# Letting a kernel's own scheduler choose the engine of its copies and relus

## The chip, the cores and the metric

The kernel runs on one core of a Trainium2 chip. A core has five engines that run side by side, each with its own in-order queue: TensorE (PE) for matmuls, VectorE (DVE), ScalarE (ACT), GpSimd (POOL) and SyncE (SP), which issues transfers here. Matmul results go to PSUM, eight banks of 128 partitions by 512 floats; everything else lives in SBUF. The metric is the time of one execution on the device, in microseconds (us), as a median of several runs. A profiled execution gives the span of the core, which is about two microseconds shorter than the measured time.

## The reference

Inputs are q, k, v of shape (4, 8, 768, 64), and four feed-forward weights. The kernel works in f16 with f32 sums.

```python
# attention: each query sees only the 6 best chunks of 32 keys
k_min, k_max = min and max of k over each chunk
ub   = sum_d max(q * k_min, q * k_max)            # upper bound of a chunk's scores
ub   = where(chunk is not in the future, ub, -1e9)
sel  = the 6 chunks of the largest ub
s    = where(sel and causal, q @ k.T / 8, -1e9)
attn = softmax(s) @ v                             # (4, 8, 768, 64)
# feed-forward with a spatial gate, on x = attn with its heads side by side, (4, 768, 512)
h    = relu(x @ w_in)                             # 1024 wide
u, v = halves of h
v_n  = (v - mean(v)) / sqrt(var(v) + 1e-6)
v_s  = w_spatial @ v_n + b_spatial                # over the 768 positions
out  = (u * v_s) @ w_out                          # (4, 768, 512)
```

## The kernel before

The kernel handles two heads at a time (a pair, 16 in all, four to a batch). For each pair there are three groups of work: `prep_ops` (transposes of keys and queries, chunk bounds, selection), `attend_ops` (scores, exponentials, attention times V, division) and, after each fourth pair, `mlp_ops` (feed-forward of a batch).

Nothing is emitted at once. Every operation is first entered with its engine, two modelled times (`occ`, how long it holds its engine, and `vis`, when its result can be seen), a priority `key` (lower is earlier) and what it reads and writes. `run` then simulates the five engines and emits the instructions in the order found:

```python
def op(self, eng, occ, vis, emit, key, r=(), w=(), take=None, drop=None, ...):
    ...                                    # dependencies from r and w
def run(self, fixed=None):
    free = {"PE": 0.8, "ACT": 2.1, "DVE": 0.8, "POOL": 1.3, "SP": 0.8}
    ...
    while left:
        best = None
        for e, lst in ready.items():
            for (k, n, t, o) in lst:       # t: when its inputs are there
                ...                        # and, if it takes a PSUM bank, when one is free
                t = max(t, free[e])
                if t < INF and (best is None or (t, k, n) < best[:3]):
                    best = (t, k, n, e, o) # earliest start, then lowest key
        ...
        if o.drop is not None:
            bank_free[j] = o.seen
```

The engine of an operation is fixed by the author. The lines that the change touches, cut to their calls:

```python
s = Schedule(banks, {"sc": 3, "tr": 2, "ub": 1, "av": 2, "mlp": 3})   # most banks of each kind

# const_ops: presets of ring buffers, and the constant rows of kh
for j in range(len(qs_r)):
    s.op("DVE", 0.8, 0.9, lambda j=j: preset(qs_r[j]), -98 + 30 * j, ...)          # L276, L277
    ...
for j in range(len(kh_r)):
    for hi in range(2):
        s.op("DVE", 0.3, 0.4, ... nc.vector.tensor_copy(kh_r[j][...], ex), -40 + 10 * j, ...)   # L303

# prep_ops(i)
s.op("PE", ..., tr_k, ...)                                     # six transposes of kp, L379
s.op("ACT", *act_cost(S), ... nc.scalar.copy(kT, bk.f16[:, 0:S]), key, ...)         # L381
...                                    # VectorE: t1, t2, kmm, chunk minima and maxima, L385 to L391
for hi in range(2):
    for par in range(2):               # spread km: VectorE if i < 2, else GpSimd, L399 and L401
        s.op("DVE" if i < 2 else "POOL", 0.2, 0.26, spread, key, ...)
for hi in range(2):
    for par in range(2):               # put kT into kh: max of a tile with itself, L409
        s.op("DVE", 0.28, 0.40, put, key + 3, ...)
s.op("PE", ..., tr_q, key + 0.3, ...)                          # L416
s.op("DVE", 0.41, 0.54, ... max(q, 0) -> rq[:, 0] ...)         # L418
s.op("DVE", 0.41, 0.54, ... max(-q, 0) -> rq[:, 1] ...)        # L421
...                                    # PE: bounds ub (L431); VectorE: mask, max8, select (L439 to L453)
# i < 5: a by six transposes on PE (L467) and a copy on VectorE (L470); later by a DMA transpose (L458)

# attend_ops(i): scores on PE (L492, triangle L495), exponentials on ScalarE (L499),
# masking of diagonal blocks on GpSimd (L507), times V on PE (L516), division on VectorE (L528),
# then x16 -> xT by PE (L544) and VectorE (L547), or by a DMA transpose (L536)

# mlp_ops(b): v = PE (L563), relu on ScalarE (L567), statistics on VectorE (L569), vn (L580)
#             u = PE (L590), relu on ScalarE (L594)
#             spatial = PE (L604), gate on VectorE (L608), gT by DMA (L612) or PE and VectorE (L619, L621)
#             out = PE (L626), copy on ScalarE (L629), DMA out (L631)

for i in range(NPAIR):
    load_ops(i, -101 if i == 0 else 10 * i - 30)
    prep_ops(i, 10 * i - (PRE if i else 50))
    attend_ops(i, 10 * i)
    ...
    if i % HP == HP - 1:
        k0 = 10 * i + 16
        mlp_ops(b, k0, k0 + 6, k0 + 14, 1.0)
```

Of the kernel before, what the change touches and what calls it, by code (L numbers as in the profile page):

```python
# [14 lines left out]
P = 128  # L15
# [42 lines left out]
class Op:  # L58
    __slots__ = ("eng", "occ", "vis", "emit", "key", "take", "drop", "deps", "left", "users", "start", "end",
                 "seen", "load", "slack", "n", "tag")  # L60


class Schedule:
# [7 lines left out]
    def op(self, eng, occ, vis, emit, key, r=(), w=(), take=None, drop=None, load=0.0, slack=0.0, tag=""):  # L71
        o = Op()
        o.eng, o.occ, o.vis, o.emit, o.key, o.take, o.drop = eng, occ, vis, emit, key, take, drop
# [15 lines left out]
        o.deps, o.left, o.users, o.start, o.end, o.seen = deps, len(deps), [], None, None, None  # L89
        for d in deps:  # L90
            d.users.append(o)
# [3 lines left out]
    def run(self, fixed=None):  # L95
# [5 lines left out]
        use = {}  # L101
        loads = 0.0
        order = []

        def push(o):
            t = 0.0
            for d in o.deps:
                t = max(t, d.end if d.eng == o.eng == "PE" else d.seen if d.eng == o.eng else d.seen + LATE)
            ready[o.eng].append((o.key, o.n, t + o.slack if o.deps else t, o))
# [4 lines left out]
        INF = 1e18  # L114
        left = len(self.ops)
        while left:
            best = None
            for e, lst in ready.items():
                for (k, n, t, o) in lst:
                    if o.take is not None:  # L120
                        c = o.take.cls
                        mine = sorted(bank_free[j] for j in range(len(holder)) if holder[j] == c)
                        cap = self.caps[c]
                        if len(mine) >= cap:
                            t = max(t, mine[len(mine) - cap])
                        t = max(t, min(bank_free))
                    t = max(t, free[e])
                    if t < INF and (best is None or (t, k, n) < best[:3]):
                        best = (t, k, n, e, o)
# [3 lines left out]
            ready[e] = [x for x in ready[e] if x[3] is not o]  # L133
            if o.take is not None:
                c = o.take.cls
# [4 lines left out]
                holder[j], bank_free[j] = c, INF  # L140
# [3 lines left out]
            o.end = t + o.occ  # L144
            o.seen = t + o.vis
            if o.load:
                loads = max(loads, o.end) + o.load
                o.seen = loads + 1.5 + (LATE_X if o.eng == "SP" else 0.0)
            free[e] = o.end
            if o.drop is not None:  # L150
                j = owner[o.drop]
                bank_free[j] = o.seen
# [7 lines left out]
        for o in order:  # L160
            o.emit()
# [23 lines left out]
def kernel(  # L185
# [31 lines left out]
    G_XBAR = 3  # L217

# [3 lines left out]
    s = Schedule(banks, {"sc": 3, "tr": 2, "ub": 1, "av": 2, "mlp": 3})  # L222
# [56 lines left out]
    def const_ops():  # L279
        s.op("DVE", 0.1, 0.2, lambda: nc.vector.memset(identity, 0.0), -100, w=["identity"])  # L280
        s.op("POOL", *pool(P), c_identity, -100.99, w=["identity"], r=["identity"])
        for j in range(2):
            s.op("DVE", 0.1, 0.2, lambda j=j: nc.vector.memset(km_r[j], 0.0), -96 + 60 * j, w=[("kmz", j)])
        s.op("DVE", 0.1, 0.2, lambda: nc.vector.memset(cmask, 0.0), -96, w=["cmask"])
        s.op("DVE", 0.1, 0.2, lambda: nc.vector.memset(tri_t, 0.0), -96, w=["tri"])
        s.op("POOL", *pool(P), lambda: nc.gpsimd.affine_select(
            out=tri_t, in_=tri_t, compare_op=Alu.is_ge, fill=NEG, base=0, channel_multiplier=-1,
            pattern=[[1, P]]), -83, r=["tri"], w=["tri"])
        s.op("DVE", 0.1, 0.2, lambda: nc.vector.memset(eps_t, 1e-6), -30, w=["eps"])
        for j in range(len(qs_r)):  # L290
            s.op("DVE", 0.8, 0.9, lambda j=j: preset(qs_r[j]), -98 + 30 * j,
                 w=[("sel", j)])
            s.op("DVE", 0.1, 0.2, lambda j=j: nc.vector.memset(v_r[j][:, :, :, D:D + 2], 1.0), -97 + 30 * j,
                 w=[("ones", j)])
        s.op("DVE", 0.86, 1.0, lambda: nc.vector.tensor_scalar(
            ex.rearrange("p (c j) -> p c j", j=CHUNK), in0=identity[0:D, 0:NCH].unsqueeze(2).to_broadcast([D, NCH, CHUNK]),
            scalar1=NEG, scalar2=None, op0=Alu.mult), -86, r=["identity"], w=["ex"])
        s.op("POOL", *pool(4), lambda: nc.gpsimd.affine_select(
            out=cmask, in_=cmask, compare_op=Alu.is_ge, fill=-1e9, base=0, channel_multiplier=1,
            pattern=[[-CHUNK, CPT]]), -84, r=["cmask"], w=["cmask"])  # L300
        for j in range(len(kh_r)):
            for hi in range(2):
                s.op("DVE", 0.3, 0.4, lambda j=j, hi=hi: nc.vector.tensor_copy(  # L303
                    kh_r[j][D * hi:D * hi + D, hi, :], ex),
                     -40 + 10 * j, r=["ex"], w=[("exrow", j, hi)])
        s.op("SP", 0.45, 2.5, lambda: nc.sync.dma_start(out=bcol, in_=moe_b_spatial.rearrange("(t p) -> p t", p=P)),
# [7 lines left out]
    def load_ops(i, key):  # L314
# [9 lines left out]
        s.op("POOL", 1.0, 0, lambda: nc.gpsimd.dma_start(out=kp, in_=view(k)), key,  # L324
             w=[("kp", i % len(kp_r))], load=PAIRB, slack=LOAD_SLACK, tag=f"ldk{i}")
        for hi in range(2):
            c0 = D * (1 - hi)
            s.op("POOL", 0.81, 0, lambda hi=hi, c0=c0: nc.gpsimd.dma_start(  # L328
                out=qs[:, :, hi, c0:c0 + D], in_=one(q, hi)), key + 0.1,
                w=[("qd", i % len(qs_r), hi)], load=PAIRB / 2, slack=LOAD_SLACK, tag=f"ldq{i}")  # L330
        s.op("POOL", 1.0, 0, lambda: nc.gpsimd.dma_start(out=vt[:, :, :, 0:D], in_=view(v)), key + 0.2,  # L331
# [4 lines left out]
    def weight_ops(key):  # L336
# [4 lines left out]
        for half in (1, 0):  # L341
            for o in range(0, NDO, 2):
                c0 = half * DH
                s.op("POOL", 0.69, 0, lambda o=o, c0=c0: nc.gpsimd.dma_start(
# [3 lines left out]
        for to in range(0, NQT, 2):  # L348
            s.op("POOL", 0.69, 0, lambda to=to: nc.gpsimd.dma_start(
# [3 lines left out]
        for o in range(0, KO, 2):  # L353
            s.op("POOL", 0.69, 0, lambda o=o: nc.gpsimd.dma_start(
# [4 lines left out]
    def spatial_ops(key):  # L359
        for so in range(NQT):  # L360
# [5 lines left out]
            s.op("PE", *pe_cost([P] * NQT), tr, key + 0.1 * so, r=["identity"] + [("ws", to) for to in range(NQT)],  # L366
                 take=bk, w=[bk])
            s.op("DVE", 0.48, 0.60, lambda so=so, bk=bk: nc.vector.tensor_copy(wsT[:, so, :], bk.f16[:, 0:S]),
                 key + 0.1 * so, r=[bk], w=[("wsT", so)], drop=bk)

    def prep_ops(i, key):
# [8 lines left out]
        s.op("PE", *pe_cost([P] * NQT), tr_k, key, r=["identity", ("kp", nk)], w=[bk], take=bk, tag=f"trk{i}")  # L380
        s.op("ACT", *act_cost(S), lambda: nc.scalar.copy(kT, bk.f16[:, 0:S]), key, r=[bk], w=[("kT", n2)], drop=bk)  # L381
        kc = kT.rearrange("d (c ch) -> d c ch", ch=CHUNK)
        t1, t2 = t1_r[n2], t2_r[n2]
        for m, op in ((0, Alu.max), (1, Alu.min)):
            s.op("DVE", 0.28, 0.40, lambda m=m, op=op: nc.vector.tensor_tensor(  # L385
                t1[:, m], in0=kc[:, :, 0:16], in1=kc[:, :, 16:32], op=op), key, r=[("kT", n2)], w=[("t1", n2, m)])
        for m, op in ((0, Alu.max), (1, Alu.min)):
            s.op("DVE", 0.16, 0.28, lambda m=m, op=op: nc.vector.tensor_tensor(
                t2[:, m], in0=t1[:, m, :, 0:8], in1=t1[:, m, :, 8:16], op=op), key, r=[("t1", n2, m)], w=[("t2", n2, m)])
        for m, op in ((0, Alu.max), (1, Alu.min)):  # L390
            s.op("DVE", 0.28, 0.40, lambda m=m, op=op: nc.vector.tensor_reduce(  # L391
                kmm[:, m, :], t2[:, m], axis=AX.X, op=op, negate=(m == 1)), key, r=[("t2", n2, m)], w=[("kmm", n2, m)])
        for hi in range(2):
            for par in range(2):
                def spread(hi=hi, par=par):
                    o = km[D * hi:D * hi + D, :, hi, :].rearrange("d m (tp r c) -> d m tp r c", r=2, c=CPT)[:, :, :, par]
                    f = kmm[D * par:D * par + D].rearrange("d m (h tp c) -> d m h tp c", h=2, c=CPT)[:, :, hi]
                    if i < 2:
                        nc.vector.tensor_tensor(o, in0=f, in1=f, op=Alu.max)  # L399
                    else:  # L400
                        nc.gpsimd.tensor_copy(o, f)  # L401
                s.op("DVE" if i < 2 else "POOL", 0.2, 0.26, spread, key, r=[("kmm", n2, 0), ("kmm", n2, 1), ("kmz", n2)],
                     w=[("km", n2, hi, par)])
        for hi in range(2):
            for par in range(2):
                def put(hi=hi, par=par):
                    o = kh[D * (1 - hi):D * (2 - hi), hi, :].rearrange("d (tp r c) -> d tp r c", r=2, c=P)[:, :, par]
                    f = kT[D * par:D * par + D].rearrange("d (h tp c) -> d h tp c", h=2, c=P)[:, hi]
                    nc.vector.tensor_tensor(o, in0=f, in1=f, op=Alu.max)  # L409
                s.op("DVE", 0.28, 0.40, put, key + 3, r=[("kT", n2)], w=[("kh", nh, hi, par)])  # L410
# [3 lines left out]
        def tr_q():  # L414
            for t in range(NQT):
                nc.tensor.transpose(bq.f16[:, t * P:(t + 1) * P], both(qs)[:, t], identity)  # L416
        s.op("PE", *pe_cost([P] * NQT), tr_q, key + 0.3, r=["identity", ("qd", nq, 0), ("qd", nq, 1)], w=[bq], take=bq, tag=f"trq{i}")
        s.op("DVE", 0.41, 0.54, lambda: nc.vector.tensor_scalar(  # L418
            rq[:, 0, P:S], in0=bq.f16[:, P:S], scalar1=0.0, scalar2=None, op0=Alu.max),
            key + 0.2, r=[bq], w=[("rq", n2, 0)])  # L420
        s.op("DVE", 0.41, 0.54, lambda: nc.vector.tensor_scalar(  # L421
            rq[:, 1, P:S], in0=bq.f16[:, P:S], scalar1=-1.0, scalar2=0.0, op0=Alu.mult, op1=Alu.max),
# [255 lines left out]
```

## Time and profile before

| | |
|---|---|
| time, median of 3 runs | 219.17 us (217.27 to 219.80) |
| span of the profiled run | 216.2 us |
| TensorE busy | 187.7 us, 87% |
| VectorE busy | 169.5 us, 78% |
| ScalarE busy | 144.8 us, 67% |
| GpSimd busy, with the issuing of loads | 104.1 us, 48% |
| moved by DMA | 27.68 MB |

Busy times are sums over the whole span, and hide that the kernel has phases: loads and the first pairs at the start, attention with feed-forward between, and the last batch's feed-forward alone at the end. So a view by stretches of the span is read before them. A row of a group gives line, engine, operation, output <- input, shapes and count, then busy time and the mean of one, then how long the engine was idle just ahead of these instructions and what ended that. L409 is line 409 of the kernel.

### The profile page before, as it was taken

What the parts mean: (1) busy time and instruction counts of PE and PEld (TensorE: products, weight loads), DVE (VectorE), ACT (ScalarE), POOL (GpSimd) and SP (SyncE); (2) the same over time, 40 slices, a digit from 0 to 9 for tenths busy, and PEclk for the clock granted to TensorE, in tenths of its full rate; (3) what the DMA queues carried; (4) which work ended last, traced back from release to release, by engine and by line L of the source; (5) the groups of instructions that cost most, each with busy time, mean ns of one, the idle gap of its engine ahead of it and who ended that gap; (6) DMA issues with size and microseconds to landing.
All of it is one profiled execution on the core that took longest, in us unless ns stands there. A gap on an engine that the chain in (4) does not pass through costs nothing.

```text
span 216.2 us, 5372 instructions
## 1 busy us (share of the span) xinstructions
PE 187.7 (87%) x1910; PEld 114.7 (53%) x1910; DVE 169.5 (78%) x604; ACT 144.8 (67%) x297; POOL 104.1 (48%) x184
## 2 busy tenths in 40 slices
PE   0269979598999899996789999999999999699991
PEld 0157867476746455654645565665555555344540
DVE  6999999799899999899899967577985422485540
ACT  2116988487879874796798793889996669374221
POOL 7999984865543683596858524125230201000000
PEclk9999999999999999999999999999999999999999
DMA  8999999998997899999999995949904644310132
GB/s 49 126 148 154 199 187 192 171 154 59 113 104 95 58 100 194 128 204 227 202 181 133 134 126 98 200 125 180 196 1 49 136 85 144 126 49 0 60 137 97
DMA packets 117306, 27.68 MB, mean 128 GB/s; under 512 B 111904, under 2 KB 114208, under 8 KB 117280
## 3 DMA queue, kind: packets, MB, share of 16 engines
q0 software_dynamic: 77200, 12.19, 79.6%
q1 hardware_dynamic: 40080, 15.15, 37.3%
q8 instruction: 15, 0.25, 0.5%
q14 instruction: 11, 0.09, 0.1%
HBM read 24.38 MB, written 6.29 MB: 142 GB/s over the span
## 4 chain that ended last, share of the span: by engine, by line
PE 59%; DVE 23%; DMA 8%; issue 4%; ACT 3%; POOL 1%; POOLq 0%; ACTq 0%; DVEq 0%
PE bank L604 12%; PE bank L492 11%; PE bank L590 8%; PE bank L563 8%; PE bank L626 7%; PE bank L516 7%; DMA vt<-in_v_dram 5%; DVE kh L409 4%; DMA a<-qs 3%; DVE m L447 3%; ACT e L499 2%; DVE t L385 2%; DVE x L528 1%; DVE rq L418 1%; DVE vn L580 1%
## 5 line engine op out<-in xcount | busy, mean ns | idle before, releaser
L499 ACT ACTIVATE e<-bank 128x512 f16<-128x512 f32 x192 | 92.8, 555 | 22.6 <-PE bank L495 10.7
L492 PE MATMUL bank<-a,kh 128*128 128x512 f16 (+3 forms) x256 | 57.3, 310 | 3.7 <-DMA a<-qs 0.8
L507 POOL TENSOR_SCALAR_AFFINE_SELECT e<-e 128x384 f16<-128x384 f16 x48 | 26.2, 545 | 57.2 <-ACT e L499 56.3
L604 PE MATMUL bank<-vn,wsT 128*128 128x512 f16 x144 | 38.1, 379 | 0.4 <-DVE vn L580 0.4
L516 PEld LDWEIGHTS <-e 128*128 128x128 f16 x672 | 28.5, 97 | 11.8 <-issue 2.4
L516 PE MATMUL bank<-vt,e 128*128 128x65 f16 x672 | 31.5, 193 | 1.3 <-POOL e L507 0.5
L492 PEld LDWEIGHTS <-kh 128*128 128x128 f16 x256 | 22.2, 99 | 18.1 <-issue 4.5
L629 ACT COPY o<-bank 128x512 f32<-128x512 f32 x24 | 14.1, 588 | 22.7 <-PE bank L626 21.6
L328 POOL DMA_DIRECT2D qs<-in_q_dram x32 | 27.0, 854 | 3.2 <-DMA a<-qs 1.1
L608 DVE SCALAR_TENSOR_TENSOR g<-bank,bcol,u 128x512 f16<-128x512 f32 x24 | 17.9, 747 | 12.4 <-PE bank L604 12.1
L409 DVE TENSOR_TENSOR kh<-kT 64x384 f16<-64x384 f16 x64 | 23.6, 369 | 2.8 <-PE bank L492 1.4
L626 PE MATMUL bank<-w_out,gT 128*128 128x512 f16 x96 | 24.5, 379 | 0.8 <-DVE gT L621 0.7
L563 PE MATMUL bank<-w_in,xT 128*128 128x512 f16 x96 | 24.3, 379 | 0.4 <-DVE xT L547 0.4
L590 PE MATMUL bank<-w_in,xT 128*128 128x512 f16 x96 | 23.6, 379 | 0.0
L381 ACT COPY kT<-bank 128x768 f16<-128x768 f16 x16 | 13.0, 811 | 11.3 <-PE bank L379 10.5
L604 PEld LDWEIGHTS <-wsT 128*128 128x128 f16 x144 | 13.0, 98 | 10.9
L331 POOL DMA_DIRECT2D vt<-in_v_dram x16 | 16.5, 1029 | 4.5 <-PE bank L431 2.7
L324 POOL DMA_DIRECT2D kp<-in_k_dram x16 | 16.7, 1043 | 3.1 <-PE bank L544 2.1
L401 POOL COPY km<-kmm 64x24 f16<-64x24 f16 x56 | 12.4, 222 | 11.9 <-DVE kmm L391 9.5
L528 DVE TENSOR_TENSOR x<-bank,rec 128x384 f16<-128x384 f32 x32 | 17.6, 549 | 0.3
L567 ACT ACTIVATE vraw<-bank 128x512 f32<-128x512 f32 x24 | 13.7, 604 | 5.9 <-PE bank L563 5.8
L569 DVE BATCH_NORM_STATS2 st<-vraw 128x6 f32<-128x512 f32 x24 | 15.5, 675 | 2.5 <-ACT vraw L567 2.4
(59 smaller groups left out, 250.4 us busy)
## 6 DMA issues: line engine op xcount, KB each, us to landing
out_dram<-o SPq DMA_DIRECT2D x24, 256.0 KB, 2.9
kp<-in_k_dram POOLq DMA_DIRECT2D x16, 192.0 KB, 5.9
qs<-in_q_dram POOLq DMA_DIRECT2D x32, 96.0 KB, 5.3
vt<-in_v_dram POOLq DMA_DIRECT2D x16, 192.0 KB, 6.0
ws_raw<-in_moe_w_spatial_dram POOLq DMA_DIRECT2D x3, 384.0 KB, 10.0
w_in<-in_moe_w_in_dram POOLq DMA_DIRECT2D x4, 256.0 KB, 6.9
w_out<-in_moe_w_out_dram POOLq DMA_DIRECT2D x2, 256.0 KB, 11.0
gT<-g SPq DMA_TRANSPOSE x18, 4.1
```

The source lines that it names most:

```text
L328: s.op("POOL", 0.81, 0, lambda hi=hi, c0=c0: nc.gpsimd.dma_start(out=qs[:, :, hi, c0:c0 + D], in_=one(q, hi)), key + 0.1, w=[("qd", i % le ...
L409: nc.vector.tensor_tensor(o, in0=f, in1=f, op=Alu.max)
L492: mm(bs.f32[:, col:col + n], lhsT=kh[:, hi, t * P:(t + 1) * P], rhs=af[:, q0 // P:(q0 + n) // P, :], start=True, stop=not dg)
L499: s.op("ACT", *act_cost(WIDTHS[g]), lambda g=g, bs=bs, e=e: nc.scalar.activation(out=e[:, BASES[g]:BASES[g] + WIDTHS[g]], in_=bs.f32[:, 0: ...
L507: nc.gpsimd.affine_select(out=o, in_=o, compare_op=Alu.is_ge, fill=0.0, base=0, channel_multiplier=-1, pattern=[[0, 3], [1, P]])
L516: mm(o[:, qi, :], lhsT=e[:, c:c + P], rhs=vt[:, hi, t, 0:D + 1], start=(part == 0 and n == 0), stop=(part == 1 and n == len(bl) - 1))
L528: nc.vector.tensor_tensor(x16[:, :, hi, :], in0=o[:, :, 0:D], in1=rec.to_broadcast([P, NQT, D]), op=Alu.mult)
L563: mm(bk.f32, lhsT=x[:, ko, t * P:(t + 1) * P], rhs=w_in_sb[:, ko, DH:DFF], start=(ko == 0), stop=(ko == NDO - 1))
L590: mm(bk.f32, lhsT=x[:, ko, t * P:(t + 1) * P], rhs=w_in_sb[:, ko, 0:DH], start=(ko == 0), stop=(ko == NDO - 1))
L604: mm(bk.f32, lhsT=wsT[:, si, t * P:(t + 1) * P], rhs=vn[:, si, :], start=(si == 0), stop=(si == NQT - 1))
L608: s.op("DVE", 0.67, 0.80, lambda t=t, bk=bk, g=g: nc.vector.scalar_tensor_tensor(out=g, in0=bk.f32, scalar=bcol[:, t:t + 1], in1=u_r[nu[t] ...
L626: mm(bo.f32, lhsT=gT[:, db, :], rhs=w_out_sb[:, db, :], start=(db == 0), stop=(db == KO - 1))
```

## The change

An operation may now be entered with a list of engines, each with its own two times. The scheduler looks at the engine on which the operation would be seen earliest, given when each engine is free, and emits it there. The aim is to take copies and relus off an engine while another is free. Beside that the feed-forward keys move up by ten (one pair), the presets of all ring buffers get the first keys, the feed-forward work may hold four banks instead of three, and the plan counts a released bank as free a quarter of a microsecond later (`LATE`).

```diff
-    def op(self, eng, occ, vis, emit, key, r=(), w=(), ...):
+    def op(self, alts, emit, key, r=(), w=(), ...):
+        o.alts = {e: (occ, vis) for e, occ, vis in (alts if isinstance(alts, list) else [alts])}
...
+                    if len(o.alts) > 1:
+                        mineend = t + o.alts[e][1]
+                        if any(f != e and max(o.at[f], free[f], now) + o.alts[f][1] < mineend for f in o.alts):
+                            continue
...
-                bank_free[j] = o.seen
+                bank_free[owner[o.drop]] = o.seen + LATE
...
+    KV, KU, KS, STEP = 26, 6, 14, 1.0
-    s = Schedule(banks, {"sc": 3, "tr": 2, "ub": 1, "av": 2, "mlp": 3})
+    s = Schedule(banks, {"sc": 3, "tr": 2, "ub": 1, "av": 2, "mlp": 4})
+    EVAC = [("DVE", 0.48, 0.60), ("ACT", 0.72, 0.87)]
+    RELU = [("ACT", 0.51, 0.65), ("DVE", 0.60, 0.74)]
+    RQ = [("DVE", 0.41, 0.54), ("ACT", 0.62, 0.76)]
+    KH = [("DVE", 0.36, 0.44), ("POOL", 0.47, 0.53), ("ACT", 0.41, 0.55)]
+    KM = [("POOL", 0.24, 0.30), ("DVE", 0.18, 0.30), ("ACT", 0.11, 0.26)]
...                                   # presets and constants
-            s.op("DVE", 0.8, 0.9, lambda j=j: preset(qs_r[j]), -98 + 30 * j,
+            s.op(("DVE", 0.4, 0.45), lambda j=j: preset(qs_r[j]), -98 + j,
-                s.op("DVE", 0.3, 0.4, lambda j=j, hi=hi: nc.vector.tensor_copy(
-                    kh_r[j][D * hi:D * hi + D, hi, :], ex),
-                     -40 + 10 * j, r=["ex"], w=[("exrow", j, hi)])
+                s.op([("ACT", 0.72, 0.87), ("DVE", 0.45, 0.58)], lambda e, j=j, hi=hi: copy(
+                    e, kh_r[j][D * hi:D * hi + D, hi, :], ex, False), -40 + 10 * j, r=["ex"], w=[("exrow", j, hi)])
...                                   # kT; likewise a, xT, wsT with EVAC, from DVE
-        s.op("ACT", *act_cost(S), lambda: nc.scalar.copy(kT, bk.f16[:, 0:S]), key, r=[bk], w=[("kT", n2)], drop=bk)
+        s.op(EVAC, lambda e: copy(e, kT, bk.f16[:, 0:S]), key, r=[bk], w=[("kT", n2)], drop=bk)
...
-                s.op("DVE" if i < 2 else "POOL", 0.2, 0.26, spread, key, ...)
+                s.op(KM, spread, key, ...)
-                s.op("DVE", 0.28, 0.40, put, key + 3, ...)
+                s.op(KH, put, key + 3, ...)
...                                   # both query relus with RQ, from DVE
...                                   # the relus of v and u and the copy of o with RELU, from ACT
-            s.op("ACT", *act_cost(512), lambda vraw=vraw, bk=bk: nc.scalar.activation(vraw, bk.f32, func=Act.Relu),
+            s.op(RELU, lambda e, vraw=vraw, bk=bk: relu(e, vraw, bk.f32),
...
-            k0 = 10 * i + 16
-            mlp_ops(b, k0, k0 + 6, k0 + 14, 1.0)
+            k0 = 10 * i + KV
+            mlp_ops(b, k0, k0 + KU, k0 + KS, STEP)
```

On VectorE a copy from SBUF is written as the maximum of a tile with itself, a copy from PSUM as a plain copy; on GpSimd and ScalarE they are plain copies.

## The prediction, made before the changed kernel ran

> **What bounds the kernel now.** I read three views: first the busy time of the engines in four stretches of the span, then the groups of instructions by shape (for the cost of one instruction), then the timeline of the first 18 us and of the tail.
>
> The stretches (columns: us, then busy time and instruction count of TensorE, its weight loads, VectorE, ScalarE and GpSimd; granted clock; DMA share; GB/s):
>
> ```profile
> 0.00:20.00 20.00, 8.67 (x76) 6.68 (x77) 17.50 (x75) 4.75 (x7) 18.80 (x27) 1.00 1.84 116
> 20.00:120.00 100.00, 89.76 (x1100) 59.50 (x1099) 94.50 (x362) 77.89 (x161) 65.57 (x120) 1.00 1.56 150
> 120.00:200.00 80.00, 77.71 (x675) 42.98 (x672) 51.86 (x161) 58.62 (x125) 19.68 (x38) 1.00 0.71 109
> 200.00:216.20 16.20, 11.51 (x70) 5.51 (x68) 5.64 (x11) 3.52 (x6) 0.00 (x0) 0.98 0.26 98
> ```
>
> The reader is to see two regimes. Up to 120 us VectorE is busy 94.5 of 100 us, with TensorE below it; from 120 us on TensorE is all but full (77.7 of 80) and VectorE is at 65%.
>
> TensorE's busy time is not its work, since a stalled matmul counts as busy. So I count columns. In the chain of waits twelve 512-column matmuls take 2.59 us, so one is 0.216 us and 1,000 columns are 0.422 us. The feed-forward part has 96 (v) + 96 (u) + 144 (spatial) + 96 (output) = 432 matmuls of 512 columns, 221,184 columns; scores 86,016; attention times V 672 x 65 = 43,680; transposes and the triangle additions 390 x 128 = 49,920; the chunk bounds 160 x 48 = 7,680. Sum 408,480 columns, 172 us at that rate. The span is 216.2, so 44 us are lost on TensorE. Counting instructions by line in each stretch puts the loss at about 16 us in the first 20, 18 us between 20 and 120, 4.5 us between 120 and 200 and 5 us in the last 16. The change can only win in these 44.
>
> What one instruction costs (columns: line, engine, operation, tiles, count | busy us, mean ns | idle before it):
>
> ```profile
> L409 DVE TENSOR_TENSOR kh<-kT 64x384 f16<-64x384 f16 x64 | 23.6, 369 | 2.8 <-PE bank L492 1.4
> L381 ACT COPY kT<-bank 128x768 f16<-128x768 f16 x16 | 13.0, 811 | 11.3 <-PE bank L379 10.5
> L401 POOL COPY km<-kmm 64x24 f16<-64x24 f16 x56 | 12.4, 222 | 11.9 <-DVE kmm L391 9.5
> L418 DVE TENSOR_SCALAR rq<-bank 128x640 f16<-128x640 f16 x16 | 7.7, 478 | 1.2 <-PE bank L416 0.7 <-ACT e L499 0.5
> L470 DVE COPY a<-bank 128x768 f16<-128x768 f16 x10 | 5.3, 547 | 0.0
> L303 DVE COPY kh<-ex 64x768 f16<-64x768 f16 x6 | 3.7, 616 | 0.1
> L567 ACT ACTIVATE vraw<-bank 128x512 f32<-128x512 f32 x24 | 13.7, 604 | 5.9 <-PE bank L563 5.8
> ```
>
> The VectorE rows hardly wait for anything (idle 0 to 3 us in a whole row): its queue is backed up, while ScalarE waits 11 us for its kT copies.
>
> The start, on VectorE, ScalarE and TensorE:
>
> ```profile
> 3.84 1.05 DVE L303 COPY kh<-ex 64x768 f16<-64x768 f16 x2
> 5.24 0.82 PE L379 MATMUL bank<-identity,kp 128*128 128x128 f16 x6 [5.24 <-DMA kp<-in_k_dram]
> 5.91 1.79 DVE L303 COPY kh<-ex 64x768 f16<-64x768 f16 x3
> 6.09 0.80 ACT L381 COPY kT<-bank 128x768 f16<-128x768 f16 x1 [4.00 <-PE bank L379]
> 7.78 0.22 DVE L276 MEMSET qs<- 128x192 uint32 x1
> 8.16 0.33 DVE L385 TENSOR_TENSOR t<-kT 128x384 f16<-128x384 f16 x1
> 16.43 0.58 PE L492 MATMUL bank<-a,kh 128*128 128x512 f16 x1 [0.63 <-DVE a L470]
> ```
>
> The first kT is complete at 6.89, but VectorE takes it up only at 8.16: constant copies and a memset that nobody needs yet are in front. The first score matmul starts at 16.43.
>
> **What the Trainium skill says.** "ScalarE: Activation LUTs", section "What ACT_TABLE_LOAD costs": an ACTIVATE with immediate scale and bias takes 186 ns + 0.833 ns per element, for any function. The trace agrees: 613 ns by that for 512 elements against 604 here. For the relu of 640 elements it gives an estimate of 719 ns alone, against 478 on VectorE. "VectorE: DVE Perf Modes", section "Why PSUM operands drop a tier": an operand in PSUM still allows two 16-bit elements a cycle, but 32-bit ones only at one. The trace agrees: 768 16-bit columns take 547 ns and 640 take 478, so 128 more cost 69 ns, 0.54 ns each. So VectorE is the faster engine for the 16-bit evacuations, and each one that moves to ScalarE costs more there than it frees. "SBUF — State Buffer", section "Who interferes with whom": a VectorE instruction with two SBUF inputs contends with a GpSimd instruction that reads SBUF. The kh copies are such instructions (written as a maximum of a tile with itself), and they spread from 332 to 616 ns in the trace, which fits; moving some of them to GpSimd makes more such meetings.
>
> **The change part by part.**
> 1. *Free choice of engine.* Movable off VectorE between 20 and 120 us (12 of the 16 pairs prepare there, 72 of 96 key transposes): kh 48 x 0.369 = 17.7; the two query relus 24 x 0.476 = 11.4; copies of a, wsT and xT about 18 x 0.546 = 9.8. Sum 38.9 of its 94.5 us. Movable off ScalarE there: kT 12 x 0.811 = 9.7, v and u relus (50 and 38 of 96 matmuls, thus 12.5 and 9.5 instructions) 22 x 0.60 = 13.2, output copies 6 x 0.588 = 3.5; so 26.4 of 77.9. GpSimd has about 34 us idle and may take kh and km, about 0.5 us for a kh copy (an estimate between km's 222 ns for 24 elements and the 545 ns of the masking of 384). If GpSimd takes some 20 kh copies, VectorE and ScalarE share (94.5 + 77.9 - 7.4) = 165 us, and ScalarE's dearer copies add about 3: 84 us each. TensorE's own work there is 82 us (100 less the loss of 18). Three engines at about 83 us in 100 can't run back to back with in-order queues; if they reach 90 to 92% of the stretch, where VectorE reached 94.5 alone, it shrinks to 91 us. Gain 9, and I take 7.5 because the loads may not follow (below).
> 2. *The start.* Of the six constant copies (3.7 us on VectorE at 616 ns) about two go to ScalarE, which is idle till 6.09; the others become two-input maxima, about 0.46 us each. VectorE is then free near 5.4, takes the first kT itself at 6.1 (0.55 instead of 0.80) and starts the chunk maxima near 6.7 instead of 8.16: 1.5 us. The query relus, at 9.53 and 10.66, may split over two engines: up to 0.5 more. But pair 1's keys land only at 10.95 whatever VectorE does, so I count 1.5 of the 2.
> 3. *Lag by ten keys more.* Feed-forward work yields to attention a pair longer. No instruction is added. TensorE's work is moved toward the end, where it fills the waits for the last pair: TensorE idles there 0.95, 0.44 and 0.51 us at 184 to 187. Gain 0.5 to 1.5; what follows the last pair, 24 + 24 + 36 + 24 matmuls of 512 columns = 23 us plus the drain, stays.
> 4. *The fourth feed-forward bank, and the later release of a bank in the plan (a quarter of a microsecond).* These change the order alone. Within the noise of the sum; I count 0.5.
> Sum: 7.5 + 1.5 + 1 + 0.5 = 10.5 us off 219.2, so 208.7; I say 208.5.
>
> **The rivals.**
> *The loads become the bound.* DMA share is 1.56 in the busy stretch, and rows of 256 bytes of input make small packets. In the first 20 us the loads of four pairs (0.59 MB each as written) move at 116 GB/s: 5 us a pair with nothing else running. At 16 pairs that is 81 us, and the weights and the transposes share the engines. If attention is to run faster, the loads have to come earlier, and they come from GpSimd's queue, which now also carries copies. In favour: one piece of the chain of waits is a V load of 10.98 us at 30.24. Against: elsewhere in the chain DMA is small, and the share falls to 0.71 afterwards. If it holds, only the start and the tail gain: 214 to 217.
> *The plan misjudges the hardware.* The order is fixed from modelled durations, in-order on each engine. A copy that goes to ScalarE behind a row of exponentials, or to GpSimd behind a 1 us load issue or a masking, comes late, and the whole chain of the pair behind it waits. For: masking waits 56 us for exponentials in the page's groups, so GpSimd stands still at places the plan must guess. Against: the plan's figures are near the trace (0.36 for kh against 0.369, 0.48 for 768 columns against 0.547). It would give 219 to 224.
> *Everything balances, better than I assume.* If the stretch falls to TensorE's own rate, as from 120 us on (77.7 of 80), the loss of 18 drops to 4: about 202.
>
> **Range and chances.** Middle 208.5. The low side is the last rival, short of its end, 201.5; the high side is the loads' case, 216. Faster by over 2% means below 214.8: I give it 0.81; within 2% 0.13; slower 0.06.
>
> **What would show it.** Right: VectorE's busy share between 20 and 120 us below 90%, ScalarE's above 80%, kh copies on two or three engines; the first score matmul near 14.5 to 15; TensorE's total of instructions unchanged and its full regime starting near 110 instead of 120; the last pair's normalisation before 178 instead of 185.2. Wrong: VectorE still over 94% (the copies stayed, or ScalarE's feed-forward relus came over in their place); waits of TensorE for loads of keys or V that are longer than now (first rival); ScalarE or GpSimd copies named as what TensorE waits for (second).

## The result and the profile after

| | time, median | runs | range |
|---|---|---|---|
| before | 219.49 us | 4 | 217.27 to 222.15 |
| changed | 207.32 us | 4 | 204.54 to 213.05 |

The ratio is 0.9398, with a 95% interval of 0.9223 to 0.9574. (All ratios here leave out executions more than 1.5% above the fastest of their kernel, two of these four and four of the six below; medians and ranges have them all.) Later, six more executions of the same kernel (e11 below) had a median of 209.33 us, 204.90 to 213.54, and a ratio of 0.9461 (0.9388 to 0.9534). By the ratios the change takes 5 to 6% off, 12 to 13 us; by the medians 12.2 us here and 8.9 in the later set (209.33 against 218.18). So a figure "against the changed kernel" below can shift by some 3 us with the executions that it is taken from. The change also widens the spread: 9 us from the fastest to the slowest, where the kernel before has 5, and under 3 in its 41 later executions.

The stretches of the changed kernel; columns as before: us, then busy time and count of TensorE, its weight loads, VectorE, ScalarE and GpSimd; granted clock; DMA share; GB/s.

```profile
0.00:20.00 20.00, 9.27 (x92) 7.23 (x93) 15.14 (x71) 10.06 (x19) 18.26 (x29) 1.00 1.68 106
20.00:120.00 100.00, 93.60 (x1137) 62.19 (x1134) 90.36 (x337) 88.62 (x195) 75.40 (x116) 1.00 1.74 156
120.00:200.00 80.00, 79.97 (x677) 44.15 (x676) 58.12 (x172) 50.31 (x108) 22.45 (x41) 1.00 0.66 114
200.00:206.30 6.30, 2.22 (x14) 0.97 (x12) 0.69 (x2) 1.76 (x3) 0.00 (x0) 1.00 0.33 125
```

Between 20 and 120 us VectorE and ScalarE now carry about the same, near 90 of 100 us each, where they had 94.5 and 77.9. From 120 to 200 us TensorE has no idle left. And the last row is 6 us long instead of 16.

Where the copies went, in the groups by shape:

```profile
L241 POOL COPY kh<-kT 64x384 f16<-64x384 f16 x42 | 22.1, 525 | 6.3 <-DVE kT L243 3.3 <-DVE rec L555 0.8 <-ACT kT L239 0.2
L239 ACT COPY kh<-kT 64x384 f16<-64x384 f16 x18 | 9.2, 509 | 5.8 <-DVE kT L243 5.5
L243 DVE COPY kT<-bank 128x768 f16<-128x768 f16 x13 | 7.2, 552 | 4.6 <-PE bank L415 4.4
L249 ACT ACTIVATE rq<-bank 128x640 f16<-128x640 f16 x16 | 10.9, 707 | 1.5 <-PE bank L449 0.9 <-DVE rq L251 0.6
L421 DVE TENSOR_TENSOR t<-kT 128x384 f16<-128x384 f16 x32 | 12.6, 422 | 0.4 <-ACT kT L239 0.2
L424 DVE TENSOR_TENSOR t<-t 128x192 f16<-128x192 f16 x32 | 9.6, 330 | 0.0
```

The count behind the shape says who got what: of 64 kh copies 42 run on GpSimd, 18 on ScalarE and 4 on VectorE; 13 of the 16 kT copies went the other way, from ScalarE to VectorE; of 32 query relus 16 are on ScalarE.

To see where the time came from I count TensorE's columns as in the prediction (1,000 columns are 0.422 us) and take them off each stretch. What is left is TensorE's loss; a matmul is counted in the stretch in which it starts. The columns of this table are the kernels of the experiments below, one profiled execution each. The last one is a second execution of the changed kernel.

| loss of TensorE, us | before | lag alone (e3) | engines fixed (e1) | old lag (e2) | changed | changed (e11) |
|---|---|---|---|---|---|---|
| 0 to 20 | 16.0 | 16.0 | 15.9 | 14.9 | 15.3 | 13.6 |
| 20 to 60 | 8.2 | 7.6 | 10.0 | 7.1 | 6.9 | 11.4 |
| 60 to 120 | 9.7 | 8.5 | 8.6 | 8.0 | 5.8 | 3.9 |
| 120 to 200 | 4.5 | 1.2 | 1.1 | 6.5 | 1.6 | 1.1 |
| after 200 | 5.4 | 4.5 | 5.4 | 4.4 | 4.3 | 4.5 |
| sum | 43.8 | 37.8 | 41.0 | 40.9 | 33.9 | 34.5 |
| last pair divided, starts at | 185.2 | 177.0 | 180.6 | 183.6 | 172.8 | 173.3 |

The prediction had the loss fall by 10.5 us; it fell by 9.9, as the span did. The two executions of the changed kernel split it quite differently between 20 and 120 us, so these two rows are best read together: 17.9 us before, 16.1 with the lag alone, 15.1 with the old lag, 18.6 with engines fixed, 12.7 and 15.3 in the changed kernel. What stands clear of such differences is the row from 120 to 200 us: 1.1 to 1.6 us with the longer lag, 4.5 and 6.5 without. (With the longer lag the later experiments have up to 2.6, and 4.0 in e4 and e7.) That the two changes need each other is to be read from the times of the experiments, more than from single rows.

### The profile page after: what moved, and what is told of

Same layout as the page of the kernel before. It is cut to its first block, busy times and chain, and to the rows that moved or that the text cites. A ratio compares the mean times of both kernels' runs of the same rounds, so it can differ in the third digit from the quotient of the medians.

```text
span 206.3 us, 5375 instructions
## 1 busy us (share of the span) xinstructions
PE 185.1 (90%) x1910; PEld 114.5 (56%) x1910; DVE 164.3 (80%) x578; ACT 150.8 (73%) x323; POOL 116.1 (56%) x184
## 4 chain that ended last, share of the span: by engine, by line
PE 62%; DMA 20%; ACT 5%; POOL 5%; DVE 4%; issue 2%; POOLq 0%; ACTq 0%
PE bank L635 13%; PE bank L523 11%; PE bank L657 10%; PE bank L621 10%; PE bank L594 7%; DMA qs<-in_q_dram 7%; PE bank L547 6%; DMA kp<-in_k_dram 6%; DMA a<-qs 4%; ACT e L530 4%; DMA gT<-g 3%; DVE vn L611 2%; PE bank L449 2%; POOL kh L241 1%; PE bank L415 1%
## 5 line engine op out<-in xcount | busy, mean ns | idle before, releaser
L523 PE MATMUL bank<-a,kh 128*128 128x512 f16 (+3 forms) x256 | 59.2, 309 | 2.2 <-DMA a<-qs 1.3
L538 POOL TENSOR_SCALAR_AFFINE_SELECT e<-e 128x384 f16<-128x384 f16 x48 | 25.6, 532 | 38.3 <-ACT e L530 37.5
L635 PE MATMUL bank<-vn,wsT 128*128 128x512 f16 x144 | 37.4, 379 | 0.0
L547 PE MATMUL bank<-vt,e 128*128 128x65 f16 x672 | 32.5, 193 | 2.3 <-ACT e L530 1.5
L239 ACT COPY o<-bank 128x512 f32<-128x512 f32 x22 | 12.9, 586 | 19.6 <-PE bank L657 15.4
L241 POOL COPY kh<-kT 64x384 f16<-64x384 f16 x42 | 22.1, 525 | 6.3 <-DVE kT L243 3.3
L657 PE MATMUL bank<-w_out,gT 128*128 128x512 f16 x96 | 24.2, 379 | 1.1 <-DMA gT<-g 1.1
L621 PE MATMUL bank<-w_in,xT 128*128 128x512 f16 x96 | 25.0, 379 | 0.0
L594 PE MATMUL bank<-w_in,xT 128*128 128x512 f16 x96 | 24.8, 379 | 0.0
L635 PEld LDWEIGHTS <-wsT 128*128 128x128 f16 x144 | 13.1, 98 | 10.9
L600 DVE BATCH_NORM_STATS2 st<-vraw 128x6 f32<-128x512 f32 x24 | 15.9, 675 | 1.8 <-ACT vraw L249 1.8
L415 PE MATMUL bank<-identity,kp 128*128 128x128 f16 x96 | 9.0, 236 | 7.1 <-DMA kp<-in_k_dram 7.1
L657 PEld LDWEIGHTS <-gT 128*128 128x128 f16 x96 | 8.9, 98 | 11.4 <-DMA gT<-g 2.1
L478 DVE MAX8 m<-bank 128x8 f32<-128x8 f32 (+4 forms) x160 | 14.4, 162 | 0.2
```

The costliest lines, as they stand in the source:

```text
L523: mm(bs.f32[:, col:col + n], lhsT=kh[:, hi, t * P:(t + 1) * P], rhs=af[:, q0 // P:(q0 + n) // P, :], start=True, stop=not dg)
L538: nc.gpsimd.affine_select(out=o, in_=o, compare_op=Alu.is_ge, fill=0.0, base=0, channel_multiplier=-1, pattern=[[0, 3], [1, P]])
L547: mm(o[:, qi, :], lhsT=e[:, c:c + P], rhs=vt[:, hi, t, 0:D + 1], start=(part == 0 and n == 0), stop=(part == 1 and n == len(bl) - 1))
L594: mm(bk.f32, lhsT=x[:, ko, t * P:(t + 1) * P], rhs=w_in_sb[:, ko, DH:DFF], start=(ko == 0), stop=(ko == NDO - 1))
L621: mm(bk.f32, lhsT=x[:, ko, t * P:(t + 1) * P], rhs=w_in_sb[:, ko, 0:DH], start=(ko == 0), stop=(ko == NDO - 1))
L635: mm(bk.f32, lhsT=wsT[:, si, t * P:(t + 1) * P], rhs=vn[:, si, :], start=(si == 0), stop=(si == NQT - 1))
```

## The experiments

Two theories stood at the start. The prediction's: the free choice of engines is the gain, and the lag a matter of 1 us. Its rival: the lag is the main part.

**e1: engines fixed.** In the changed kernel each operation is held on its engine of before (the others get a time that they never win with).

```diff
-    KH = [("DVE", 0.36, 0.44), ("POOL", 0.47, 0.53), ("ACT", 0.41, 0.55)]
+    KH = [("DVE", 0.36, 0.44), ("POOL", 0.47, 1e6), ("ACT", 0.41, 1e6)]
...                        # likewise EVAC, RELU, RQ, KM, the constant rows; kT on ScalarE
```

> The changed kernel with every copy and relu held on the engine it had before; lag, presets, bank cap and later release stay. Theory of the prediction (the free choice is worth 7.5 to 9 of the 12 us, the lag 1): it comes back to 214 to 217 us, VectorE over 93 of the 100 us between 20 and 120. Rival (the lag is the main part, the free choice a small one): 209 to 211 us.

Measured: 214.81 us (214.0 to 215.6), ratio 0.9833 (0.9780 to 0.9886). The prediction's number: with the lag in place the free choice is worth 3.7 points of ratio against the later runs of the changed kernel, 8 us. But VectorE's share, which I said would be back over 93%, was 90.8 of 100 (third number pair of the row):

```profile
20.00:120.00 100.00, 90.62 (x1088) 61.07 (x1087) 90.78 (x339) 77.66 (x162) 63.71 (x113) 0.97 1.52 147
```

So e1 is slower without VectorE being fuller than in the changed kernel (90.4). Its trace also has two lulls of TensorE of 2.6 us, at 31.6 and 104.1 us, each with 3.4 us at half clock. These do not seem to set its time: of its four executions the two with a mean clock of 0.981 took 214.8 us on average, and so did the two with 0.992.

**e2: the old lag.**

```diff
-    KV, KU, KS, STEP = 26, 6, 14, 1.0
+    KV, KU, KS, STEP = 16, 6, 14, 1.0
```

> The changed kernel with the old feed-forward keys (lag 16 instead of 26), everything else kept. Theory of the prediction: 208 to 209 us, since the lag only fills waits in the tail. Rival (lag is the main part): 213 to 217 us, with TensorE losing time again between 120 and 200 us and at the last pair.

Measured: 217.80 us (214.44 to 225.09, 20 runs), ratio 0.9886 (0.9854 to 0.9918). The rival's case, with a median just above its range: without the lag nearly the whole gain is gone. (The profiled execution, and so the table, is one of the fastest, 214.98 us.) So the lag term is the step of the prediction that fell.

The timeline of TensorE around the last pair shows what the lag buys. First e2:

```profile
183.00 0.27 PE L547 MATMUL bank<-vt,e 128*128 128x65 f16 x3 [0.41 <-POOL e L538]
184.22 0.51 PE L575 MATMUL bank<-identity,x 128*128 128x128 f16 x6 [0.95 <-DVE x L559]
184.56 0.38 PE L594 MATMUL bank<-w_in,xT 128*128 128x512 f16 x1
185.45 0.82 PE L594 MATMUL bank<-w_in,xT 128*128 128x512 f16 x3 [0.51 <-DVE xT L243]
```

Then the changed kernel at the same point:

```profile
173.58 0.59 PE L657 MATMUL bank<-w_out,gT 128*128 128x512 f16 x2
174.01 0.50 PE L575 MATMUL bank<-identity,x 128*128 128x128 f16 x6
174.34 0.59 PE L635 MATMUL bank<-vn,wsT 128*128 128x512 f16 x2
174.78 0.59 PE L594 MATMUL bank<-w_in,xT 128*128 128x512 f16 x2
```

The brackets are idle time just ahead of a row, and the changed kernel has none. Spatial and output matmuls (L635, L657) of the batch before stand between the steps of the last pair. In e2 too few of them are left. But the brackets of e2 are 1.9 us in all, as I had counted; the larger effect is the last row of the table, a last pair that is through 11 us earlier. With feed-forward work held back, pairs get TensorE first, and the work held back fills their gaps from 120 us on (loss 6.5 us in e2, 1.6 in the changed kernel).

**e3: the lag alone, in the kernel before.**

```diff
-            k0 = 10 * i + 16
+            k0 = 10 * i + 26
```

> The kernel before with nothing but the lag raised from 16 to 26. Theory of the prediction: 218 to 219 us, about 1 us gained. Rival (lag is the main part): 209 to 213 us.

Measured: 212.47 us (211.80 to 212.57), ratio 0.9724 (0.9687 to 0.9761). The rival's number again. One constant gives 6 us, nearly half of the whole, with every instruction on its old engine.

**e5 and e6: how much lag.** The same constant at 21 and at 32, in the changed kernel.

```diff
-    KV, KU, KS, STEP = 26, 6, 14, 1.0
+    KV, KU, KS, STEP = 21, 6, 14, 1.0      # e6: 32
```

> The changed kernel with the feed-forward keys half way (lag 21). Theory now (the lag leaves feed-forward matmuls over to fill TensorE while the last pairs wait for their chains, and its worth grows till enough of them are over): between the two, 208 to 213 us, the last pair's normalisation between 173 and 184 us. Rival (each set of keys is a throw of the dice for the order, and 26 a lucky one): anything from 206 to 218 us, with no relation to where TensorE idles.

> The changed kernel with a longer lag (32). Theory now: no more to fill, so 205 to 208 us, TensorE still without idle from 160 us on. Rival (lucky throw): clearly above 208 us. Third theory (more lag only moves work into the end, where nothing runs beside it): above 210 us, with a longer stretch after the last pair's normalisation.

Measured: 217.27 us (214.80 to 220.77) with 21, and 209.68 us (206.32 to 213.22) with 32, ratio 0.9509 (0.9406 to 0.9611). The longer lag behaves nearly as my theory says: the median is above 208 us, but about the changed kernel's in its later executions (209.33), with the last pair at 171.3 us and no idle from 160 us on. The half-way lag does not: it is as slow as the old one. Only the part of the theory that speaks of the end holds for it: the loss between 120 and 200 us is 6.5, 4.4, 1.6 and 1.7 us with a lag of 16, 21, 26 and 32, but with 21 another 17.0 us go between 20 and 120 us. The worth of the lag doesn't grow evenly, and part of what a setting gives is the order that it happens to yield. How large that part is stays open.

**e7: kh copies held on VectorE.**

```diff
-    KH = [("DVE", 0.36, 0.44), ("POOL", 0.47, 0.53), ("ACT", 0.41, 0.55)]
+    KH = [("DVE", 0.36, 0.44), ("POOL", 0.47, 1e6), ("ACT", 0.41, 1e6)]
```

> The changed kernel with the kh copies held on VectorE (60 of 64 had left it, 42 to GpSimd and 18 to ScalarE); all else kept, lag 26 too. If VectorE's load up to 120 us is what the free choice relieved: 60 x 0.369 = 22 us come back to it over the 16 pairs, and the time rises by 5 to 8 us, to 211 to 214. If the free choice gains through the start and the feed-forward relus instead: within 2 us of 206.

Measured: 212.38 us (211.92 to 214.44), ratio 0.9737 (0.9671 to 0.9802), so 6 us slower than the changed kernel by the ratios (0.9737 less 0.9461, of 218 us), 3 to 5 by the medians, with VectorE at 94.5 of 100 us between 20 and 120 again. That is as expected: this one class is most of what the free choice brings.

**e8: relus and output copies held on ScalarE.**

```diff
-    RELU = [("ACT", 0.51, 0.65), ("DVE", 0.60, 0.74)]
+    RELU = [("ACT", 0.51, 0.65), ("DVE", 0.60, 1e6)]
```

> The changed kernel with feed-forward relus and output copies held on ScalarE (16 of 72 had left it for VectorE). By the balance of the two engines (about 10 of ScalarE's 151 us): at most 1.5 us slower, 205.5 to 208. If freeing ScalarE for exponentials is what counts: 209 us or more.

Measured: 215.33 us (214.77 to 216.73), ratio 0.9863 (0.9806 to 0.9920). A clear miss. Sixteen instructions that move cost 9 us by the ratios, 6 to 8 by the medians. The loss of TensorE between 20 and 60 us is 13.4 us, against 6.9 in the first profile of the changed kernel, and the first relu that had moved to VectorE starts only at 55.5 us there (the first of the group u at 65.2), so the time of the relus is not what is lost there. GpSimd's timeline of e8 shows what is:

```profile
39.84 1.02 POOL L367 DMA_DIRECT2D vt<-in_v_dram  x1 [1.07 <-PE bank L526]
40.86 0.71 POOL L390 DMA_DIRECT2D w_out<-in_moe_w_out_dram  x1
42.41 0.71 POOL L390 DMA_DIRECT2D w_out<-in_moe_w_out_dram  x1 [0.85 <-DVE bank L470]
...
44.26 1.01 POOL L360 DMA_DIRECT2D kp<-in_k_dram  x1 [0.59 <-DMA ws_raw<-in_moe_w_spatial_dram]
...
46.15 0.82 POOL L364 DMA_DIRECT2D qs<-in_q_dram  x1 [0.33 <-DMA ws_raw<-in_moe_w_spatial_dram]
47.45 0.82 POOL L364 DMA_DIRECT2D qs<-in_q_dram  x1 [0.48 <-DMA kp<-in_k_dram]
48.26 1.02 POOL L360 DMA_DIRECT2D kp<-in_k_dram  x1
49.27 1.03 POOL L367 DMA_DIRECT2D vt<-in_v_dram  x1
54.09 0.83 POOL L364 DMA_DIRECT2D qs<-in_q_dram  x1 [3.79 <-DMA vt<-in_v_dram]
...
56.24 0.53 POOL L538 TENSOR_SCALAR_AFFINE_SELECT e<-e 128x384 f16<-128x384 f16 x1
```

The load of queries at 54.09 waits 3.79 us for the V load that was issued at 39.84 and took 14 us to land. It needs nothing of that V. But it is the eighth load after it, and the trace records the semaphore of each load: the 73 loads use eight of them (99 to 106) in turn, and this load waits for number 100, which that V load holds. It is so in every trace here, the kernel before included: no load starts before the eighth load ahead of it has landed, and 0.28 us more have passed. So GpSimd's queue stands still while eight of its loads are under way, by the program's own semaphores, and what is behind in the queue stands too: the masking at 56.24, which TensorE waits for. TensorE in this time (us, busy time and count, granted clock, DMA share, GB/s):

```profile
50.00:52.00 2.00, 2.00 (x27) 1.00 1.52 159
52.00:54.00 2.00, 0.24 (x8) 1.00 1.74 156
54.00:56.00 2.00, 0.00 (x0) 0.57 2.62 153
56.00:58.00 2.00, 1.17 (x7) 0.50 2.93 151
58.00:60.00 2.00, 2.00 (x16) 0.50 2.58 150
60.00:62.00 2.00, 2.00 (x19) 0.72 0.70 44
```

A lull of 4.6 us (52.24 to 56.83). The clock goes to half at 54.29, still inside it, and stays there until 61.11, so the matmuls of another 4.3 us run at half clock: a 512-column matmul takes 634 ns there instead of 379. The Trainium skill has this in "TensorE: Matmul & The Clock Gate", section "What's actually happening": after an idle window of some 3.4 us the clock goes to half, until a busy one has passed. The granted clock of 0.50 in these rows agrees. The window need not be idle throughout, though: TensorE had been idle for only 2.0 of the 3.4 us before the drop, and the measurement decides. A late load is paid for twice.

How much of e8's time this is stays open. The second profile of the changed kernel (e11) has a shorter standstill in the same place and loses 11.4 us between 20 and 60 us, yet its span is 8.2 us shorter than e8's. Of these 8.2 us only 2.0 lie between 20 and 60 us; 3.6 lie between 60 and 120 us, where the relus or the order may be the reason.

**e4: half the loads.** From pair 4 on only one of two heads of keys and V and half of the query rows are loaded; the rest of the buffers keeps old data, so the output is not the reference's.

```diff
-        ... nc.gpsimd.dma_start(out=kp, in_=view(k)), key,
+        ... nc.gpsimd.dma_start(out=kp if i < 4 else kp[:, 0], in_=view(k) if i < 4 else one(k, 0)), key,
...                        # likewise vt; qs[:, 0:3] of each head
```

> The changed kernel, from pair 4 on loading only one of the two heads' keys and V and half of the query rows (the rest of the buffers keeps old data), same order of instructions. If the loads bound the changed kernel between 20 and 120 us: 200 to 203 us, with the waits for keys and queries of 10 us gone. If they do not, and the loss is in the order and the balance of engines: within 1.5 us of 206.

Measured: 203.67 us (202.89 to 205.16), ratio 0.9336 (0.9282 to 0.9389). Against the changed kernel's later runs (0.9461) that is 2.7 us, by the medians 4 to 6. Between the theories: the loads cost some 3 us or more. But TensorE's waits for keys and queries are not gone, as the first theory had it: 7.8 us in all against 9.5, and 5.7 of them are the first load's. The spread is smaller, 2.3 us against 9 in the changed kernel, but e7 and e12, with all the loads, have only 2.5 and 1.7, so it does not show the loads' part.

**e9 and e10: weights later.** If the weights' loads stand in the pairs' way at 34 to 57 us, later ones should help. In e9 only their keys move, and that of the spatial weight's transposes; e10 does the same to e8.

```diff
-    weight_ops([22, 23, 26, 27, 28, 29, 30, 31, 32])
+    weight_ops([30, 31, 36, 37, 44, 47, 50, 64, 66])
-            spatial_ops(38)
+            spatial_ops(56)
```

> The changed kernel with the weights' load keys and the transposes of the spatial weight moved later, and nothing else. Theory (at 34 to 57 us the weights stand in front of the pairs' loads; when one of those lands late GpSimd's queue stands still, TensorE idles for some microseconds and then runs at half clock): 202 to 206 us and a narrower spread than the changed kernel's 204.5 to 213. Rival (the weights are needed anyway, and the wait moves to the first feed-forward matmuls): 206 to 210 us.

> The run with relus held on ScalarE (215.3 us), now with the weights later as well. If its 9 us came from the lull of TensorE at 52 to 56 us and the half clock after it, and not from the relus: 204 to 209 us. If the relus on ScalarE are what costs: 213 us or more.

Measured: e9 215.17 us (214.89 to 216.21), ratio 0.9882 (0.9844 to 0.9920); e10 216.36 us (211.73 to 219.24). Both misses. GpSimd's timeline of e9 shows why:

```profile
40.37 1.01 POOL L360 DMA_DIRECT2D kp<-in_k_dram  x1 [0.55 <-DMA w_in<-in_moe_w_in_dram]
56.37 0.70 POOL L390 DMA_DIRECT2D w_out<-in_moe_w_out_dram  x1 [5.21 <-DMA kp<-in_k_dram]
```

The loads changed places, and the queue stood still all the same, now 5.2 us behind keys that took 16 us to land, with TensorE idle or at half clock from 52.5 to 63.5 us. (The mean clock of the profiled execution is 0.976, those of the other five 0.971 to 0.976, so they probably had the same.) So e9 shows the full queue again, and refutes that these keys avoid it. e10 has the same lull and says nothing of the relus: whether they cost anything beside it stays open.

**e11: the changed kernel again.**

> The changed kernel unchanged, for more executions on the same chip as the two runs above: 204 to 208 us in most, some near 212; the slow ones at a lower mean clock of TensorE, if the lull at 50 us is what comes and goes.

Measured: 209.33 us (204.90 to 213.54), with only two of the six between 204 and 208. Its profiled execution has the same wait of queries for V, 2.3 us long and ending at 52.5 us. TensorE idles for 3.2 us, but its clock stays at 1.00:

```profile
52.00:54.00 2.00, 0.16 (x6) 1.00 1.80 107
54.00:56.00 2.00, 0.65 (x8) 1.00 2.22 105
```

So the changed kernel runs close to the edge at which e8 falls off. The fastest executions had a mean clock of 1.000 (204.90) and 0.999 (207.43), the slowest 0.980 (213.54); but one of 210.11 had 0.982 and one of 212.37 had 0.992. In e2, with 20 executions, it is plainer: 1.000 at 214.44 and 214.98 us, 0.972 to 0.985 in the five above 222. This fits a lull that comes and goes, but only the profiled executions show it directly.

**e12: three feed-forward banks, and banks counted free at once.**

```diff
-                bank_free[owner[o.drop]] = o.seen + LATE
+                bank_free[owner[o.drop]] = o.seen
-    s = Schedule(banks, {"sc": 3, "tr": 2, "ub": 1, "av": 2, "mlp": 4})
+    s = Schedule(banks, {"sc": 3, "tr": 2, "ub": 1, "av": 2, "mlp": 3})
```

> The changed kernel with three feed-forward banks instead of four and banks counted free at once, as before. The prediction's fourth term (0.5 us): 206 to 207.5 us. Rival (the plan without the quarter microsecond promises banks too early, and TensorE stalls on them): 209 us or more.

Measured: 210.25 us (209.39 to 211.06), ratio 0.9648 (0.9601 to 0.9694). By the ratios the two are worth 4 us here, the rival's number; by the medians of the same chip (210.25 against 209.33) it is 0.9 us. And e1 and e3 differ by these two, the presets, the plan's corrected durations and the rewritten loop of `run`, and there the kernel that has them is the slower one (0.9833 against 0.9724). So neither size nor sign is settled, and no cause is shown.

No version that ran was faster than the changed kernel with its full work.

## Why the prediction was right, and where it was not

**What bounds the kernel.** Right in the main. Taking kh copies off VectorE (e7 undoes that) is worth 6 us by the ratios, 3 to 5 by the medians. But e1 is slower than e7 with VectorE at 90.8 of 100 us, where e7 has 94.5, so VectorE's share alone does not set the time. ScalarE above 80%: 88.6. VectorE below 90%: 90.4, just missed.

**Step 1, free choice, 7.5 us.** Right in size, 8 us by e1, but only with the longer lag. With the old lag it brings 2.5 us by the ratio and 0.5 by the medians, and that with presets and banks counted in (e2). GpSimd's 0.5 us for a kh copy was 0.525. What the step left out: the copies that left slow VectorE down. The chunk maxima, which read two SBUF tiles, take 348 and 248 ns in e1:

```profile
L423 DVE TENSOR_TENSOR t<-kT 128x384 f16<-128x384 f16 x32 | 10.2, 348 | 1.0 <-ACT kT L239 0.8
L426 DVE TENSOR_TENSOR t<-t 128x192 f16<-128x192 f16 x32 | 6.9, 248 | 0.0
```

In the changed kernel they take 422 and 330, as shown above: 32 x 74 + 32 x 82 ns is 5 us of VectorE given back against e1, and 3 us against the kernel before, where they take 361 and 294. Single instructions of the changed kernel show whose doing it is: of the first kind the 12 with no GpSimd computing beside them take 367 ns on average, the 19 that overlap a kh copy on GpSimd 461; of the second kind 20 take 260 and 11 take 435. This is the contention with GpSimd's reads that the prediction named from the Trainium skill, and didn't put a number on. VectorE's busy time fell by only 5 us in all (169.5 to 164.3), for a second reason as well: some 32 us of copies and query relus left it, but 24 us came over in exchange, 13 kT copies (7.2 us), 24 more km copies (5.8) and the 16 feed-forward relus and output copies (10.9).

**Step 2, the start, 1.5 us.** VectorE takes up the first chunk maxima at 6.94, predicted near 6.7. The first scores come at 15.81 in this execution, not at 14.5 to 15. The timeline of the changed kernel:

```profile
3.51 1.67 ACT L239 COPY kh<-ex 64x768 f16<-64x768 f16 x2 [1.42 <-DVE ex L332]
6.94 0.62 DVE L421 TENSOR_TENSOR t<-kT 128x384 f16<-128x384 f16 x2
7.13 0.84 POOL L364 DMA_DIRECT2D qs<-in_q_dram  x1
8.02 1.07 POOL L241 COPY kh<-kT 64x384 f16<-64x384 f16 x2
9.03 0.83 POOL L364 DMA_DIRECT2D qs<-in_q_dram  x1
13.73 0.80 PE L449 MATMUL bank<-identity,qs 128*128 128x128 f16 x6 [1.22 <-DMA qs<-in_q_dram]
14.32 1.48 PE L498 MATMUL bank<-identity,qs 128*128 128x128 f16 x12
15.81 0.58 PE L523 MATMUL bank<-a,kh 128*128 128x512 f16 x1
```

Two kh copies on GpSimd now stand between the two query loads of pair 1. The second goes out at 9.03 instead of directly behind the first (8.10 in the kernel before), lands at 13.6, and the transposes of pair 0's selected queries (L498) stand behind pair 1's (L449) in TensorE's queue. So 0.7 us of loss was saved here. In e11 that load went out at the same time and landed at 12.4, the first scores came at 15.1 and the loss was 13.6, a gain of 2.4. So the landing makes more of a difference here than the place of the two copies. This execution is the outlier: in the ten other traces with a free choice (all but e1 and e3) the first scores come at 14.6 to 15.4 and the loss is 13.6 to 14.9, a gain of 1.1 to 2.4 us. The step was right. The presets had no part in it: with engines fixed (e1) the loss is 15.9.

**Step 3, the lag, 1 us.** Wrong in size, and the step that failed: "Feed-forward work yields to attention a pair longer ... Gain 0.5 to 1.5". It measured 6 us alone (e3) and 9 us with the free choice (e2, 0.9886 less 0.9461). I counted only the three waits that I could see in the tail, 1.9 us. I did not ask what the pairs gain when they come first: the last one is through 8 us earlier in e3, and what waits behind fills TensorE from 120 us on. That stretch has 3.3 of the 6 us of e3 and 4.9 of the 7.0 us between the profiled spans of e2 and the changed kernel. Whether the rest is the lag's, or the order that a setting happens to yield (as e5 makes one think), is not shown.

**Step 4, banks and their release, 0.5 us.** Undoing both costs 4 us by the ratios and 0.9 by the medians (e12), and with engines fixed the sign may turn. Not settled.

**The sum.** 10.5 us predicted, 12.2 measured. The terms, each undone alone, come to 8, 9 and 4 us: more than the whole, since free choice and lag need each other. Added alone they come to less than the whole: by the ratios everything but the lag brings 2.5 us (e2) where 9.5 were predicted, the lag 6 (e3) where 1 was, and about 3 of the 11.8 us come only with both, where nothing was. Errors of -7, +5 and +3 us happened to cancel. That the total came out right was luck; its split was wrong.

**The rivals.** "The loads become the bound" holds in part: 3 us or more (e4). "The plan misjudges the hardware" came true in part in e8 and e9, where a shift of order that the plan allows ran into a full load queue. That the plan was near the trace in durations, which I gave as evidence against, says nothing of the landing times of loads.

## What to carry to other kernels

In a statically ordered kernel two levers on the same idle time need not add: here freeing the busy engine paid 2.5 us alone, and 8 us once independent work was held back to fill what opens. So try them together, and undo each alone to see its share. Before moving a copy onto the engine that also issues the loads, look at its queue, and at how many loads the program lets be under way (eight here): a load or a masking behind a blocked issue is late by the whole block. And keep TensorE from idling for 2 us and more in mid-kernel, as it may then pay at half clock as well.

## What was not expected of the hardware

- GpSimd's queue stood still at the eighth load after one that had not landed, for 3.8 us in e8 and 5.2 us in e9; loads took 14 and 16 us to land there, with a median of 7.0 for V loads in e8. The reason is in the traces: the loads use eight semaphores of the program in turn. What more of them would bring was not tried.
- In e8 TensorE was granted 0.50 of its clock from 2.1 us into its lull on, for 6.8 us. The seven such stretches in mid-kernel, in e1 (two), e5, e6, e8, e9 and e10, last 3.4, 6.8 or 10.2 us. In the 3.4 us before each of them TensorE had been idle for 2.0 to 2.6 us; a lull of 2.3 us in the kernel before and one of 3.2 us in e11 passed without.
- VectorE maxima with two SBUF inputs were 21 and 33% slower in the changed kernel than in e1 (348 to 422 ns and 248 to 330), and slow just where they met kh copies on GpSimd (461 and 435 ns, against 367 and 260 alone).
- A relu of 512 32-bit PSUM columns takes 683 ns on VectorE and 599 on ScalarE, one of 640 16-bit columns 478 and 707: which engine is the faster one depends on the type.
